# A gated feed-forward layer on one core: a half weight chunk loaded on another DMA queue, and a wide subtraction in three parts

## The chip, the cores and the metric

One core of a Trainium2 chip runs the whole layer in one launch. The metric is the device time of one execution in microseconds. Five engines work side by side, each through its own list of instructions in order: TensorE (PE, matmuls; its weight loads are shown as PEld), VectorE (DVE), ScalarE (ACT), GpSimd (POOL) and SyncE (SP). SyncE and ScalarE also issue the DMA transfers, each on its own queue; an instruction of a list that waits holds up those behind it.

## The reference

x is 2048 x 1024, w_gate and w_up are 1024 x 3584, w_down is 3584 x 1024, all bfloat16:

```
def reference(x, w_gate, w_up, w_down):
    return (gelu(x @ w_gate) * (x @ w_up)) @ w_down      # gelu in its tanh form
```

## The kernel before

The tokens are taken in two halves of 1024 (`for h in range(NH)`, line 972 on), each as two blocks of 512. For a half, the first products give hT, the gelu of the gate times the up product, with the 3584 hidden features on the partitions in 28 tiles of 128; the down products then turn hT into output.

**Products by sums.** The products are not made plainly but in a scheme of seven partial products (Winograd's form of Strassen's), which needs sums and differences of blocks of both factors. A "pair" joins two tiles of 128 features; with the two halves of the contraction and the two blocks of tokens that is a 2 x 2 product of blocks. Its seven products are called m1 to m7. The sums of the weights (s1 to s4, and a22, a plain copy) are made by `s_sum`, on GpSimd for most, on ScalarE for a22, on VectorE for s3 (`s3_both`); the sums of the tokens (t1 to t4, b22) once for a half. In the down products the same is done with hT (`s_down`) and w_down (`t_down`).

**Order of a half.** `quads` (line 498) takes a list of pairs. Per pair PE runs m6, m5, m7, m3, m4 for gate and up, 40 matmuls of 128 x 128 by 128 x 512; while it does so, the sums of the next pair are made (`prep`). m1 and m2 of a pair, plain bfloat16 matmuls of the weight blocks themselves, run ahead of that. The dictionaries `thens` hang further work behind a product of a pair: `thens[7]["m5"]` is done once the code of m5 of the eighth pair has been written, `"start"` before the pair's first product. Each engine's instructions run in the order in which they are written (`on`), so a place in `thens` is a place in each engine's list.

In the first half the order is: `first_units`, a couple of two pairs (MID), the eight LEADS pairs (their m1 and m2 were made in `first_units`), and then the couples from `begin` = 10 on: pairs 10 and 11, then 12 and 13. A couple starts with m1 of both pairs, for each gate then up, so 4 x 4 bfloat16 matmuls, and m2 of both in the same way. "The couple" below is pairs 10 and 11. The second half has seven couples.

**Weight chunks.** `load_w` (line 198) loads columns of w_gate (j = 0) or w_up (j = 1) for a chunk of 512 features, four tiles or two pairs. Chunks lie in two places in turn of `w_mem`, or in still unused parts of hT. Chunk 5 belongs to the couple of pairs 10 and 11: its first half (256 columns) to pair 10, its second to pair 11. It takes the memory of chunk 1, whose second half is read last by the sums of the eighth LEADS pair, which are made during the seventh. Chunk 6 belongs to pairs 12 and 13 and takes the memory of chunk 3. `load_half` (line 1016) loads half a chunk in two transfers, gate then up, 512 KB each; `load_chunk` (line 980) loads a whole one in two of 1024 KB. Both are issued on ScalarE's queue in this stretch.

**What else is on SyncE's queue there.** Two things. (a) The second half's first token block is transposed by DMA into hT, 128 x 512 at a time (`stage_x`, line 736, called through `run_x`, two at a time; six of the eight follow each other in the eighth pair), and stored to DRAM (`store_x`, line 742). (b) The sums t2 and t4 of w_down are made once and kept in DRAM: `stage_load` (line 702) loads two rows' blocks of w_down, `stage_step` (line 719) subtracts on VectorE into one of two buffers in `o_mem`, and line 722 stores the buffer to `t_dram`. A step that writes a buffer waits until the store that reads it has landed.

**A transfer's semaphore.** Each transfer takes the next of eight semaphores in turn, over both queues, and is not issued before the transfer that last used it has landed.

**The down products.** `down_group` starts with m1, 28 bfloat16 matmuls, and then m5, 28 matmuls whose right sides are the 14 blocks of t1, in order, two matmuls a block. For the first group of a half the t1 blocks are made in the last pair's `thens` (lines 1097 to 1121) by `t_down` on VectorE, whose last argument says how many blocks one instruction does: two by default, and six (128 x 3072 elements) for blocks 8 to 13 in the last call (line 1120). The six-block instruction (line 691) is the last of t1; behind it stand the seven in-place subtractions of s2 (line 765).

Of the kernel before, what the change touches and what calls it, by code (L numbers as in the profile page):

```python
# [34 lines left out]
def kernel(  # L35
# [14 lines left out]
    KD = D // P  # L50
# [18 lines left out]
    NS = KF // 2  # L69
# [60 lines left out]
    def sp(inst):  # L130
        return on("sp", inst)

    def act(inst):
        return on("act", inst)

    def dve(inst):
        return on("dve", inst)
# [60 lines left out]
    def load_w(key, j, k0, k1, queue=sp, f0=0, f1=FG):  # L198

        c0 = key[1] * FG  # L200
        eng = nc.scalar if queue is act else nc.sync
        src = (wgv, wuv)[j][:, k0:k1, c0 + f0 : c0 + f1]
        queue(eng.dma_start(out=chunks[key][j][:, k0:k1, f0:f1], in_=src))  # L203
# [24 lines left out]
    FA = 2 * P  # L228
# [391 lines left out]
    def wd_rows(i0, i1):  # L620

        assert i1 <= 8 or i0 >= 8
        e0 = 2 * CH + i0 * D if i1 <= 8 else (i0 - 8) * D
        return w_mem[:, e0 : e0 + (i1 - i0) * D].rearrange("p (a b) -> p a b", b=D)

    def b22_blocks(i0, i1):

        assert i1 <= 4 or i0 >= 4
        e0 = (NS - 8) * D + i0 * DN if i1 <= 4 else 4 * CH + (i0 - 4) * DN
        return w_mem[:, e0 : e0 + (i1 - i0) * DN].rearrange("p (a b) -> p a b", b=DN)  # L630
# [24 lines left out]
    def right(grp, name, i0, i1):  # L655

        r0 = ((grp * len(SEQ) + SEQ.index(name)) * NS + i0) % NR
        assert r0 + i1 - i0 <= NR
        t = t_mem[:, r0 * DN : (r0 + i1 - i0) * DN]
        return t.rearrange("p (a b) -> p a b", b=DN)  # L660
# [16 lines left out]
    def t_down(grp, name, i0, i1, step=2):  # L677

        for i in range(i0, i1, step):
            t = right(grp, name, i, i + step)  # L680
            rows = wd_rows(i, i + step)
            b11, b12 = rows[:, :, 0:DN], rows[:, :, DN:D]
            if name in ("t2", "t4"):
                src = t_dram[:, i : i + step, 0 if name == "t2" else 1, :]
                sp(nc.sync.dma_start(out=t.bitcast(F32), in_=src))
            elif name == "b22":
                act(nc.scalar.copy(out=t, in_=b22_blocks(i, i + step)))
            else:
                b22 = b22_blocks(i, i + step) if name == "t3" else None
                in0, in1 = (b12, b11) if name == "t1" else (b22, b12)  # L690
                dve(nc.vector.tensor_tensor(out=t, in0=in0, in1=in1, op=ALU.subtract))  # L691
# [280 lines left out]
    for h in range(NH):  # L972
        hT = hT0 if h == 0 else hT_pool.tile([P, KF, SH], BF16, name="hT")
        begin = 0
        if h == 0:
# [4 lines left out]
            def load_chunk(key):  # L980
                if key[1] * PPG < NPAIR and key not in chunks:
                    new_chunk(key)
                    for j in range(2):
                        load_w(key, j, 0, KD, act)
# [19 lines left out]
        def run_loads():  # L1004
            while loads and first_step(loads[0]) <= nstep - len(steps):
                stage_load(loads.pop(0))
# [6 lines left out]
        if h == 0:  # L1013
            run_loads()

            def load_half(c, f0):
                if f0 == 0:
                    new_chunk((0, c))
                for j in range(2):
                    load_w((0, c), j, 0, KD, act, f0, f0 + FA)  # L1020

            thens = [
                {
                    "start": [
                        lambda: s_sum(0, MID[0], 0, "a22"),
                        lambda: s_sum(0, MID[0], 1, "a22"),
                        lambda: run_steps(1),
                    ],
                    "m5": [lambda: load_half(3, 0)],
                    "m3": [lambda: run_steps(1)],  # L1030
                    "m4": [lambda: new_x(1), lambda: run_steps(1), run_loads],
                },
                {
                    "m5": [lambda: load_half(3, FA)],
                    "m7": [lambda: fetch_to(QB, 0)],
                    "m3": [lambda: run_steps(1), run_loads],
                },
            ]
            quads(hT, h, MID, (h, LEADS[0]), thens, False, True, True)
            thens = [{} for _ in LEADS]  # L1040
            for n in range(NL):
                thens[n]["start"] = []
                thens[n]["m3"] = [lambda: run_steps(1), run_loads]
            for n in range(NL // 2):
                thens[2 + n]["start"].append(run_x)
            thens[1]["m5"] = [lambda: load_half(4, 0)]
            thens[3]["m5"] = [lambda: load_half(4, FA)]
            thens[5]["m5"] = [lambda: load_half(5, 0)]
            thens[7]["m5"] = [lambda: load_half(5, FA)]
            thens[5]["m7"] = [lambda: load_chunk((0, 6))]  # L1050
            thens[7]["start"].append(run_x)
            thens[7]["m4"] = thens[7]["m3"] + [run_x]
            thens[7]["m7"], thens[7]["m3"] = [run_x], [run_x]
            quads(hT, h, LEADS, (h, begin), thens, True, False, True)
            s_late.append(
                shared_pool.tile([P, NL // 2 * TB], F32R, name="s_late")
            )
            run_late()

        for lead in range(begin, NPAIR, PPG):  # L1060
            members = range(lead, lead + PPG)
            thens = [{} for _ in members]

            def add(n, name, *fs):
                thens[n].setdefault(name, []).extend(fs)

            add(1, "m3", lambda key=(h, lead // PPG + 2): load_chunk(key))
            if h == 0:
                add(0, "m1", lambda: run_steps(2 if lead == begin else 1), run_loads)
                add(0, "start", lambda: run_steps(1), run_loads)  # L1070
                for n in range(PPG):
                    add(n, "m3", lambda: run_steps(1), run_loads)
                    add(n, "m4", run_late)
                if lead == begin:
                    add(0, "m5", lambda: store_x(hT0, 0, KH))
                    add(0, "m3", lambda: store_x(hT0, KH, KD))
                    add(0, "m4", run_late)
            for n, pair in enumerate(members):
                if pair == NPAIR - 2 - (h == 0):
                    add(  # L1080
                        n,
                        "start" if h else "m7",
                        lambda: load_wd_rows(0, 4),
                        lambda: load_wd_rows(4, 8),
                    )
                if h > 0 and 6 < pair < 11:
                    i = s3_late[pair - 7]
                    at = "start" if n == 0 else "m3"
                    add(n, at, lambda i=i: s_down(hT, 0, "s3", i, i + 2))
                if pair < NPAIR - 1:  # L1090
                    continue
                add(
                    0,
                    "m1",
                    lambda: early.append(wd_pool.tile([P, WDT, D], BF16, name="wd_sb")),
                    lambda: s_down(hT, 0, "s3", 0, 4, 4),
                )
                if h == 0:
                    add(0, "m1", lambda: run_steps(1), run_loads)
                add(  # L1100
                    n,
                    "start",
                    lambda: load_b22(4, NS),
                    lambda: load_wd_rows(8, 10),
                    lambda: load_wd_rows(10, 12),
                    lambda: load_wd_rows(12, NS),
                    lambda: load_b22(0, 4),
                )
                add(n, "m6", lambda: t_down(0, "t1", 4, 6))
                add(n, "m7", lambda: s_down(hT, 0, "s1", 4, 8, 4))  # L1110
                add(n, "m7", lambda: s_down(hT, 0, "s1", 0, 4, 4))
                add(n, "m3", lambda: t_down(0, "t1", 0, 2))
                add(
                    n,
                    "m4",
                    lambda: t_down(0, "t2", 0, NT2),
                    lambda: t_down(0, "t1", 2, 4),
                    lambda: t_down(0, "t1", 6, 8),
                    lambda: s_down(hT, 0, "s1", 8, NS, 6),
                    lambda: t_down(0, "t1", 8, NS, 6),  # L1120
                )
            nxt = (h, lead + PPG) if lead + PPG < NPAIR else None
            quads(hT, h, members, nxt, thens, lead == 0)
# [78 lines left out]
```

## Time and profile before

| | us |
|---|---|
| median of 3 runs | 540.74 |
| lowest, highest | 540.11, 541.68 |
| the profiled execution | 542.03 |
| its span, first to last instruction | 540.3 |
| PE busy in it | 532.3 |

The granted clock of TensorE is 1.000 over the span. Moments are given in microseconds from the span's start. In the views, L511 is the line of the pairs' matmuls, L793 that of the down products' matmuls; "w_mem<-in_w_up_dram" reads: written is w_mem, read is w_up. A row of the timeline gives start, duration, engine, line, operation, tiles, shapes, the count of instructions merged into it, and in brackets the idle time before and what ended it. A row of the waits gives the total in us, the number of waits and the longest.

### The profile page before, as it was taken

To read this page: it belongs to the slowest core of one execution; us is meant where nothing else is said; L and a number is where in the kernel's file an instruction comes from. 1 tells how busy PE (TensorE), PEld (TensorE's weight loads), DVE (VectorE), ACT (ScalarE), POOL (GpSimd) and SP (SyncE) were. 2 spreads that over 40 slices of the span, in tenths; PEclk is the share of its full clock that TensorE was granted. 3 is DMA by queue.
4 is the path that set the end of the run, shared out by engine and by line. 5 is a ranking of instruction groups with operands and counts; after the bars stand their busy time and mean duration, and the time that the engine had idled before them with its cause. 6 is when DMAs were issued, how large, how long until landed. Compare 5 with 4: busy or idle time off the path is not lost.

```text
span 540.3 us, 6965 instructions
## 1 busy us (share of the span) xinstructions
PE 532.3 (99%) x2360; PEld 382.1 (71%) x2380; DVE 374.8 (69%) x453; ACT 273.8 (51%) x471; POOL 256.7 (48%) x202
## 2 busy tenths in 40 slices
PE   9999999999899999999999999999999999999997
PEld 4448888876577676767768676776768686866866
DVE  0399988989599998889565253434444569969951
ACT  4466666656454319216465555556555551452270
POOL 0079999997399300000045494948677670000000
PEclk9999999999999999999999999999999999999999
DMA  8974747399982896789950413314050329677845
GB/s 221 249 269 118 234 153 183 90 296 195 288 287 106 293 341 226 252 267 307 324 189 4 153 51 107 103 54 150 7 156 13 143 86 339 217 246 241 292 143 209
DMA packets 97747, 102.69 MB, mean 190 GB/s; under 512 B 18224, under 2 KB 72624, under 8 KB 97712
## 3 DMA queue, kind: packets, MB, share of 16 engines
q1 hardware_dynamic: 71248, 82.52, 48.2%
q10 hardware_dynamic: 26464, 19.73, 12.9%
q8 instruction: 19, 0.31, 0.2%
q14 instruction: 16, 0.13, 0.1%
HBM read 85.98 MB, written 12.58 MB: 182 GB/s over the span
## 4 chain that ended last, share of the span: by engine, by line
PE 95%; DMA 4%; issue 1%; DVE 0%; ACT 0%; DVEq 0%; ACTq 0%
PE bank L511 57%; PE bank L793 33%; PE bank L355 5%; DMA w_mem<-in_w_up_dram 2%; DMA hT<-in_w_gate_dram 1%; DMA t_dram<-o_sb 1%; DMA w_mem<-in_x_dram 1%; DVE o_sb L719 0%; DVE hT L318 0%; ACT o_sb L849 0%; DVEq L318 0%; ACTq L203 0%
## 5 line engine op out<-in xcount | busy, mean ns | idle before, releaser
L511 PE MATMUL bank<-t_mem,s_mem 128*128 128x512 f32 x1096 | 252.5, 391 | 0.0
L511 PEld LDWEIGHTS bank<-t_mem,s_mem 128*128 128x128 f32 x1096 | 205.6, 188 | 44.2 <-ACT bank L572 0.9
L462 POOL TENSOR_TENSOR s_mem<-w_mem 128x512 fp32r<-128x512 bf16 x80 | 100.4, 1274 | 180.6 <-DVE t_mem L300 95.5
L318 DVE TENSOR_TENSOR hT<-w_mem,bank 128x512 bf16<-128x512 f32 x106 | 71.2, 683 | 73.2 <-PE bank L511 43.5
L527 DVE TENSOR_TENSOR bank<-bank,m 128x512 f32<-128x512 f32 x112 | 72.4, 693 | 45.2 <-ACT m L567 42.7
L793 PE MATMUL bank<-t_mem,s_mem 128*128 128x512 f32 x416 | 98.8, 394 | 0.1
L313 ACT ACTIVATE w_mem<-bank 128x512 f32<-128x512 f32 x106 | 62.8, 596 | 59.1 <-DVE bank L527 35.7
L793 PEld LDWEIGHTS bank<-t_mem,s_mem 128*128 128x128 f32 x416 | 78.0, 188 | 18.0 <-DVE t_mem L691 0.9
L511 PE MATMUL bank<-xT,w_mem 128*128 128x512 bf16 x311 | 70.5, 379 | 3.0 <-DMA w_mem<-in_w_up_dram 2.5
L462 POOL TENSOR_TENSOR s_mem<-w_mem,s_mem 128x512 fp32r<-128x512 bf16 x46 | 65.6, 1448 | 3.4 <-PE bank L511 3.4
L691 DVE TENSOR_TENSOR t_mem<-w_mem 128x1024 fp32r<-128x1024 bf16 (+1 forms) x52 | 65.7, 1307 | 0.4 <-PE bank L511 0.4
L511 PEld LDWEIGHTS <-w_mem 128*128 128x128 bf16 x320 | 30.5, 98 | 40.8 <-DMA w_mem<-in_w_up_dram 3.0
L462 POOL TENSOR_TENSOR s_mem<-s_mem,w_mem 128x512 fp32r<-128x512 f32 x46 | 55.7, 1231 | 0.2
L572 ACT COPY bank<-bank 128x512 f32<-128x512 f32 x56 | 32.0, 571 | 25.8 <-PE bank L511 21.5
L475 ACT CAST s_mem<-w_mem 128x512 fp32r<-128x512 bf16 x48 | 29.5, 616 | 24.8 <-PE bank L511 23.5
L567 ACT COPY m<-bank 128x512 f32<-128x512 f32 x56 | 32.9, 588 | 16.1 <-PE bank L511 16.0
L793 PEld LDWEIGHTS <-hT 128*128 128x128 bf16 x224 | 21.3, 98 | 26.6 <-issue 2.1
L858 ACT CAST o_sb<-bank 128x512 bf16<-128x512 f32 x27 | 14.8, 585 | 33.8 <-PE bank L793 33.8
L793 PE MATMUL bank<-t_mem,s_late 128*128 128x512 f32 (+1 forms) x132 | 30.3, 382 | 0.0
L537 ACT COPY bank<-bank 128x512 f32<-128x512 f32 x40 | 22.8, 570 | 14.7 <-PE bank L511 14.7
L765 DVE TENSOR_TENSOR s_mem<-hT 128x512 fp32r<-128x512 bf16 (+2 forms) x28 | 23.0, 838 | 8.6 <-PE bank L793 8.6
L793 PEld LDWEIGHTS bank<-t_mem,s_late 128*128 128x128 f32 x132 | 24.4, 188 | 4.9
(61 smaller groups left out, 397.3 us busy)
## 6 DMA issues: line engine op xcount, KB each, us to landing
t_mem<-t_dram SPq DMA_DIRECT2D x56, 512.0 KB, 5.5
wd_sb<-in_w_down_dram SPq DMA_DIRECT2D x26, 512.0 KB, 7.3
t_dram<-o_sb SPq DMA_DIRECT2D x14, 512.0 KB, 3.2
w_mem<-in_w_gate_dram ACTq DMA_DIRECT2D x6, 1024.0 KB, 5.4
w_mem<-in_w_up_dram ACTq DMA_DIRECT2D x6, 1024.0 KB, 7.9
w_mem<-in_w_gate_dram SPq DMA_DIRECT2D x8, 512.0 KB, 6.0
w_mem<-in_w_up_dram SPq DMA_DIRECT2D x8, 512.0 KB, 7.3
w_mem<-in_w_down_dram SPq DMA_DIRECT2D x4, 1024.0 KB, 6.7
```

The source lines that it names most:

```text
L313: act(nc.scalar.activation(out=g_sb, in_=ps[:], func=ACT.Gelu_apprx_tanh))
L318: nc.vector.tensor_tensor(out=hT[:, fc, tb * TB : (tb + 1) * TB], in0=g_sb, in1=ps[:], op=ALU.mult,)
L355: nc.tensor.matmul(banks[held[u][j]][:], lhsT=w_sb[:, kd, f0 : f0 + P], rhs=xT[0][:, kd, :], start=kd == 0, stop=kd in (KH - 1, KD - 1), s ...
L462: pool(nc.gpsimd.tensor_tensor(out=t, in0=in0, in1=in1, op=op))
L475: act(nc.scalar.copy(out=t, in_=a(1, 1)))
L511: nc.tensor.matmul(banks[bank][:], lhsT=lhs[:, c, :], rhs=rhs[:, c, :], start=start and c == 0, stop=c == KH - 1, skip_group_check=True,)
L527: nc.vector.tensor_tensor(out=banks[dst][:], in0=banks[src][:], in1=m5[:], op=ALU.add)
L567: act(nc.scalar.copy(out=m5[j][:], in_=banks[V_[j]][:]))
L572: act(nc.scalar.copy(out=banks[R_[j]][:], in_=banks[Q_[j]][:]))
L691: dve(nc.vector.tensor_tensor(out=t, in0=in0, in1=in1, op=ALU.subtract))
L765: dve(nc.vector.tensor_tensor(out=t, in0=in0, in1=in1, op=op))
L793: nc.tensor.matmul(banks[bank][:, c0:c1], lhsT=lhs(i, u), rhs=rhs(i)[:, c0:c1], start=start and i == 0, stop=stop and i == NS - 1, skip_gr ...
```

## The change

`load_half` gets the queue as an argument. The second half of chunk 5 is issued on SyncE's queue at the start of the eighth LEADS pair, ahead of that pair's first transposes, and no longer on ScalarE's after that pair's m5. Chunk 6 is issued on ScalarE's queue after m5 of the seventh pair, no longer after m7 of the sixth. And the last `t_down` call of t1 does two blocks an instruction, three instructions in place of one, in both halves of the tokens. The order of all other instructions on PE, DVE, ACT and POOL stays.

```diff
-            def load_half(c, f0):
+            def load_half(c, f0, queue=act):
                 if f0 == 0:
                     new_chunk((0, c))
                 for j in range(2):
-                    load_w((0, c), j, 0, KD, act, f0, f0 + FA)
+                    load_w((0, c), j, 0, KD, queue, f0, f0 + FA)
...
             thens[5]["m5"] = [lambda: load_half(5, 0)]
-            thens[7]["m5"] = [lambda: load_half(5, FA)]
-            thens[5]["m7"] = [lambda: load_chunk((0, 6))]
+            thens[7]["start"].append(lambda: load_half(5, FA, sp))
+            thens[6]["m5"] = [lambda: load_chunk((0, 6))]
             thens[7]["start"].append(run_x)
...
                     lambda: s_down(hT, 0, "s1", 8, NS, 6),
-                    lambda: t_down(0, "t1", 8, NS, 6),
+                    lambda: t_down(0, "t1", 8, NS),
```

## The prediction

> **What bounds the kernel now.** I read the page's first rows, then the chain of work that ended last, then the waits by engine, then the timelines around the places these point at.
>
> ```profile
> span 540.3 us, 6965 instructions
> PE 532.3 (99%) x2360; PEld 382.1 (71%) x2380; DVE 374.8 (69%) x453; ACT 273.8 (51%) x471; POOL 256.7 (48%) x202
> ```
>
> The span is TensorE's: 532.3 of 540.3 us. Only the 8.0 us in which PE has nothing to multiply can be won, and the edit removes no matmul. Which of these 8 us does it touch? The waits name two candidates.
>
> ```profile
> PE bank L511 <- DMA w_mem<-in_w_up_dram: 2.5, 1, 2.5
> PEld bank L793 <- DVE t_mem L691: 0.9, 2, 0.5
> ```
>
> The first is one wait of 2.5 us for a load of w_up, the second two waits of the weight load for the helper whose call is split, one in each half of the tokens. The chain shows where the first comes from (start, duration, what):
>
> ```profile
> 124.95 3.17 DMA t_dram<-o_sb
> ...
> 128.14 0.02 ACTq L203
> ...
> 128.20 8.86 DMA w_mem<-in_w_up_dram
> ...
> 137.10 22.89 PE bank L511 x101
> ```
>
> The up half of the couple's second half chunk is issued at 128.20, only after a store on SyncE's queue has landed (124.95 to 128.12), takes 8.86 us, and PE starts as it lands. The PE timeline gives the hole's size:
>
> ```profile
> 99.73 32.25 PE L511 MATMUL bank<-t_mem,s_mem 128*128 128x512 f32 x139
> 131.82 2.76 PE L511 MATMUL bank<-xT,w_mem 128*128 128x512 bf16 x11
> 137.10 4.49 PE L511 MATMUL bank<-xT,w_mem 128*128 128x512 bf16 x20 [2.52 <-DMA w_mem<-in_w_up_dram]
> 141.25 18.52 PE L511 MATMUL bank<-t_mem,s_mem 128*128 128x512 f32 x80
> ```
>
> The third row's 20 matmuls at 0.38 us each overlap: (4.49 - 0.38) / 19 = 0.216 us from start to start. The last matmul before the hole ends at 131.82 + 2.76 = 134.58, so starts at 134.20, and the next was due at 134.42. It starts at 137.10: the stall costs **2.68 us**. By the same pace the gate half, which feeds the four matmuls just before, is needed at 134.42 - 4 x 0.216 = 133.56.
>
> **The change part by part.** What issues when, on ScalarE's queue (first six rows) and on SyncE's (the rest):
>
> ```profile
> 107.94 0.37 ACTq L203 DMA_DIRECT2D w_mem<-in_w_gate_dram  x1
> 108.41 0.77 ACTq L203 DMA_DIRECT2D w_mem<-in_w_up_dram  x1
> 109.82 1.58 ACTq L203 DMA_DIRECT2D w_mem<-in_w_gate_dram  x1
> 111.44 2.22 ACTq L203 DMA_DIRECT2D w_mem<-in_w_up_dram  x1
> 126.63 0.37 ACTq L203 DMA_DIRECT2D w_mem<-in_w_gate_dram  x1
> 128.20 0.39 ACTq L203 DMA_DIRECT2D w_mem<-in_w_up_dram  x1
> ...
> 116.81 0.38 SPq L702 DMA_DIRECT2D wd_sb<-in_w_down_dram  x1
> 124.95 0.37 SPq L722 DMA_DIRECT2D t_dram<-o_sb  x1
> 125.42 10.03 SPq L736 DMA_TRANSPOSE hT<-in_x_dram  x6
> 135.54 0.53 SPq L722 DMA_DIRECT2D t_dram<-o_sb  x1
> ...
> 137.33 2.54 SPq L736 DMA_TRANSPOSE hT<-in_x_dram  x2
> ```
>
> *The half chunk moves to SyncE's queue.* Its two issues (the fifth and sixth row) now stand between the store at 124.95 and the six transposes. They read and write the same memory, so they wait for the same last GpSimd subtraction, which already let the queue go on here (the transposes start at 125.42 with no gap after the store). The gate half is then issued at 125.42 and the up half near 125.8, 1.2 and 2.4 us earlier, and ahead of the transposes, where until now the up half was issued beside the third of them. In the built program the up half no longer waits for the store's landing but for a transfer issued near 108, long over.
>
> When does it land? The rates of two-microsecond stretches (last two columns: share of the DMA engines, GB/s):
>
> ```profile
> 121.00:123.00 2.00, 2.00 (x11) 1.65 (x10) 2.00 (x2) 2.00 (x5) 2.00 (x2) 1.00 1.07 369
> 131.00:133.00 2.00, 1.95 (x10) 1.07 (x10) 2.00 (x5) 1.73 (x4) 2.00 (x2) 1.00 1.39 276
> 133.00:135.00 2.00, 1.58 (x8) 0.50 (x6) 2.00 (x3) 1.36 (x3) 0.28 (x1) 1.00 1.55 67
> ```
>
> Undisturbed loads move at some 350 GB/s (the first row, taken 5% lower). The whole chunk comes one pair later, near 118, so from there to the end of the half chunk lie one w_down load (0.52 MB), the whole chunk (2.10), the store (0.52) and the half chunk (1.05): 4.19 MB, 12.0 us at 350 GB/s. The way there and back adds some 1.6, what the smallest store takes in all:
>
> ```profile
> out_dram<-o_sb SPq DMA_DIRECT2D x1, 64.0 KB, 1.6
> ```
>
> That is **131.6**. The other bound comes from the nearest like transfers, the half chunks (512 KB) and the whole chunk (1024 KB) of this stretch, median us from issue to landing:
>
> ```profile
> w_mem<-in_w_gate_dram ACTq DMA_DIRECT2D x2, 512.0 KB, 5.6
> w_mem<-in_w_up_dram ACTq DMA_DIRECT2D x2, 512.0 KB, 8.7
> w_mem<-in_w_gate_dram ACTq DMA_DIRECT2D x1, 1024.0 KB, 10.1
> w_mem<-in_w_up_dram ACTq DMA_DIRECT2D x1, 1024.0 KB, 13.0
> ```
>
> Up half 125.8 + 8.7 = 134.5, gate half 125.4 + 5.6 = 131.0: against 134.42 and 133.56, so even that leaves 0.1 us. I take 131.6, nearer to what the order in the queue gives; the stall goes whole: **-2.68 us** (bounds -2.6 and -2.68 by these rows, 0 and a loss by the rivals).
>
> A page speaks against this. The Trainium skill, DMA: Bandwidth & Descriptors, section "Issuing engines are not separate DMA queues", says that DMAs of either engine run on the same 16 DMA engines and interleave, whoever started them, so that another issuing engine saves little but sequencer time. By it the change of queue as such would bring nothing, only the earlier issue and the place ahead of the transposes; the third rival gives its time.
>
> *The whole chunk, one pair later.* Its two issues took 1.58 and 2.22 us (third and fourth row) behind the unfinished half chunk of 107.94, and held ScalarE's queue up to 113.66. One pair later nothing is ahead of them, and 0.4 us each is likely. ScalarE gains up to 3 us there, PE nothing: the 139 matmuls from 99.73 run without an idle entry at (32.25 - 0.39) / 138 = 0.231 us, against (18.52 - 0.39) / 79 = 0.230 in the stretch from 141.25. The bound is 138 x 0.001 = 0.2 us; I take 0. The chunk is first read, by the preparation of the pair after next, in the couple's second pair, half way through the 80 matmuls from 141.25, near 150.5; issued at 118 and at the 13.0 us of its row it lands by 132. That is cover enough.
>
> *What is queued behind on SyncE.* Two issues of 0.4 us push the six transposes, the store and the load behind them by 0.8 us. Who waits for these? VectorE, in its subtraction of the staged w_down, which writes a buffer that the store of 135.54 reads:
>
> ```profile
> 142.31 1.22 DVE L719 TENSOR_TENSOR o_sb<-wd_sb,o_sb 128x1024 fp32r<-128x1024 bf16 x1
> 145.00 0.70 DVE L527 TENSOR_TENSOR bank<-bank,m 128x512 f32<-128x512 f32 x1 [1.48 <-ACT m L567]
> ```
>
> ```profile
> t_dram<-o_sb SPq DMA_DIRECT2D x1, 512.0 KB, 4.2
> ```
>
> The last row is that store: 135.54 + 4.2 = 139.8. PE needs the sum of 145.00 at its 25th matmul after 141.25, near 146.9; in the changed kernel, 2.68 earlier, 144.2. So the sum must start by 143.5, the subtraction by 142.3, and the store must have landed then: 2.5 us later than now, against 0.8 of issue. Cost 0; the first rival prices what lies beyond.
>
> *One subtraction split in three* (both halves of the tokens, from line 1120). First its duration and that of the narrow form, then the first place where PE waits for it:
>
> ```profile
> L691 DVE TENSOR_TENSOR t_mem<-w_mem 128x1024 fp32r<-128x1024 bf16 x50 | 59.0, 1225 | 0.4 <-PE bank L511 0.4
> ```
>
> ```profile
> 191.19 3.35 DVE L691 TENSOR_TENSOR t_mem<-w_mem 128x3072 fp32r<-128x3072 bf16 x1
> 462.50 3.48 DVE L691 TENSOR_TENSOR t_mem<-w_mem 128x1024 fp32r<-128x1024 bf16 x3
> ...
> 190.55 4.03 PE L793 MATMUL bank<-t_mem,s_mem 128*128 128x512 f32 x16
> 194.59 5.58 PEld L793 LDWEIGHTS bank<-t_mem,s_mem 128*128 128x128 f32 x25 [0.44 <-DVE t_mem L691]
> ```
>
> The wide one ends at 194.54, and the 17th weight load starts at 194.59: rows 8 to 13 of t1 were all one wait. Three narrow ones in a row take 3.48 us, as at 462.50: the first is done at 191.19 + 1.22 = 192.4, the second at 193.6, the third at 194.7. PE wants the 17th matmul at 190.55 + 16 x 0.230 = 194.2, the 21st at 195.2, the 25th at 196.1: none waits. The matmul was due at 194.2 and could start at 194.6, and a weight load that stands idle 0.44 us leaves the next one uncovered too; I take **0.3 us** for each place, between 0 and 0.45. VectorE works 0.13 us longer; its next subtractions, seven in 4.3 us, stay ahead of a PE that uses a pair in 0.9. Two places: **-0.6 us**.
>
> **Sum:** 2.68 + 0.6 = 3.3 us. The profiled execution took 542.03 us (span 540.3 and 1.7 around it), so the changed one would take 538.7. The median of the three runs is 540.74, 1.29 lower. If profiling adds these 1.29 to any run, the median goes to 537.4. But the last rate row shows 67 GB/s against 276 just before: the landing at 137.06 includes a pause of about (276 - 67) x 2 / 276 = 1.5 us, which other runs need not have; then their stall is nearer 1.2 to 1.4, the gain 1.8 to 2.0, and the median 538.7 to 538.9. The three runs' spread, 540.11 to 541.68, is as wide as such a pause. I stand between, at the side of the pause: **538.4 us**, own range 537.3 to 539.2.
>
> **The rivals.**
> 1. *SyncE's queue becomes late.* If the transposes can't be issued until the half chunk has drained (131.6), six at 1.3 us end at 139.4 (the last row of SyncE's queue: two took 2.54; the six here took 10.03, their end in the pause), the store lands at 143.6 and the subtraction misses its 142.3 by 1.3 us. For it: an issue behind queued work did stretch (2.22 us at 111.44). Against it: these transposes were issued beside the half chunk too. Price 1.3, net -2.0: 538.7 to 540.0.
> 2. *The stall is small in ordinary runs* (the edit does what it says, where little is to be had). With the pause and the slow stretch after it gone, the up half lands at 135 and the stall is 0.6; with the split's 0.6 the gain is 1.2: 539.5. For it the 67 GB/s row; against it the range of three runs.
> 3. *The half chunk shares the engines as before.* From the gate's issue to the up half's landing it took 137.06 - 126.63 = 10.43 us; from 125.42 that is 135.85, and 1.43 us of stall stay. Net -1.25 - 0.6: 540.2 in the profiled run's terms, 538.9 to 540.2. By the Trainium skill (DMA: Bandwidth & Descriptors, "Issuing engines are not separate DMA queues") this is the case. The trace, with an up half issued beside the third transpose, can't tell.
> 4. *Slower: the whole chunk gets in front.* It is now issued at 118, not 110, so the half chunk may find 2.1 MB ahead of it. The up half at the 13.0 us that the whole chunk's up part took behind other loads lands at 125.8 + 13.0 = 138.8: a stall of 4.4 for 2.68, less 0.6, is +1.1: 541.8. It decides from a landing at 137.7 on; at over 0.3% only from 139.3 on. Against it: by the volumes above the whole chunk is through at 127.
>
> **How the numbers follow.** Forecast 0.62, rival 1 0.08, rival 2 0.14, rival 3 0.08, rival 4 0.08. A measurement of this kernel can tell about 0.3%, 1.6 us, from no change: the bounds are 539.1 and 542.4. Nearly all of the forecast, with half of rival 1, is faster: 0.64. Rivals 2 and 3, the rest of rival 1 and part of 4: same, 0.30. Slower 0.06. The range goes from 537.2 to 540.3: it leaves out rival 4 and the edges.
>
> **What would show it.** Right: no PE wait for w_up left near 134; the up half's landing before 134.4; no weight load waiting for L691; three L691 rows of 1.2 us in place of one of 3.35; PE idle time down from 8.0 to about 5 us. Wrong: a wait of PE or the weight load at 134 to 148 for w_gate, w_up or for VectorE behind a store; a landing after 134.4; the m5 of the down stage waiting for a later subtraction.

## The result and the profile after

The changed kernel takes 537.68 us (median of 6 runs, 537.35 to 539.00), the kernel before beside it 541.49 (6 runs, 540.11 to 543.21): a ratio of 0.9935, 95% interval 0.9914 to 0.9955. The profiled execution took 538.38 us for 542.03.

The first rows of the page after, then PE's waits:

```profile
span 536.6 us, 6968 instructions
...
PE 531.6 (99%) x2360; PEld 382.4 (71%) x2380; DVE 375.8 (70%) x457; ACT 274.2 (51%) x471; POOL 257.9 (48%) x202
```

```profile
PE bank L245 <- PEq L1186: 0.8, 1, 0.8
PE bank L793 <- DMA t_mem<-t_dram: 0.2, 1, 0.2
```

PE runs the same 2360 matmuls; 5.0 us are idle in place of 8.0, and w_up is no longer among its waits. The timeline of PE (start, duration, count) shows where the hole was:

```profile
99.77 31.89 PE L511 MATMUL bank<-t_mem,s_mem 128*128 128x512 f32 x140
131.51 7.08 PE L511 MATMUL bank<-xT,w_mem 128*128 128x512 bf16 x31
138.24 18.51 PE L511 MATMUL bank<-t_mem,s_mem 128*128 128x512 f32 x80
```

m1 and m2 of the couple are one row now. From the first of these matmuls to the first of m6 it is 138.24 - 131.51 = 6.73 us, against 141.25 - 131.82 = 9.43 before. SyncE's queue, and the landing of the two halves after their issue:

```profile
125.03 0.37 SPq L722 DMA_DIRECT2D t_dram<-o_sb  x1
125.48 0.42 SPq L203 DMA_DIRECT2D w_mem<-in_w_gate_dram  x1
126.00 1.02 SPq L203 DMA_DIRECT2D w_mem<-in_w_up_dram  x1
127.07 10.23 SPq L736 DMA_TRANSPOSE hT<-in_x_dram  x6
137.40 0.53 SPq L722 DMA_DIRECT2D t_dram<-o_sb  x1
```

```profile
w_mem<-in_w_gate_dram SPq DMA_DIRECT2D x1, 512.0 KB, 5.8
w_mem<-in_w_up_dram SPq DMA_DIRECT2D x1, 512.0 KB, 7.3
```

The up half lands at 126.00 + 7.3 = 133.3, 0.8 us before PE (131.51 + 12 x 0.216 = 134.1) wants it. VectorE does meet the queue's delay, without harm:

```profile
140.92 1.23 DVE L719 TENSOR_TENSOR o_sb<-wd_sb,o_sb 128x1024 fp32r<-128x1024 bf16 x1 [1.54 <-DMA t_dram<-o_sb]
142.06 1.53 DVE L527 TENSOR_TENSOR bank<-bank,m 128x512 f32<-128x512 f32 x2
```

And the split: three narrow subtractions, and 55 weight loads beside them without an idle entry:

```profile
188.18 3.49 DVE L691 TENSOR_TENSOR t_mem<-w_mem 128x1024 fp32r<-128x1024 bf16 x3
```

```profile
187.51 12.47 PEld L793 LDWEIGHTS bank<-t_mem,s_mem 128*128 128x128 f32 x55
```

The spans differ by 3.66 us. Taking the starts of PE's instructions in each trace (first matmul of line 511, first of the couple's m1, first of its m6, first of each down stage, first of the second half's pairs) and the end of its last one cuts every execution into the same stages, and this table carries most of what follows (us):

| run | start | to the couple | m1, m2 | to down | down 1 | second half's pairs | down 2 | tail |
|---|---|---|---|---|---|---|---|---|
| before | 33.65 | 98.17 | 9.43 | 43.44 | 88.25 | 175.56 | 88.42 | 3.34 |
| changed | 33.89 | 97.62 | 6.73 | 43.43 | 87.89 | 175.56 | 88.55 | 2.91 |
| e1, split only | 33.40 | 98.22 | 10.81 | 43.45 | 87.98 | 175.58 | 88.15 | 3.34 |
| e2, half only | 33.63 | 98.23 | 6.73 | 43.43 | 88.26 | 175.56 | 88.45 | 2.93 |
| e3, chunk only | 33.59 | 97.61 | 9.97 | 43.45 | 88.25 | 175.56 | 88.45 | 3.34 |
| e4, half on ScalarE's queue | 34.01 | 97.62 | 6.73 | 43.43 | 87.89 | 175.56 | 88.10 | 3.34 |
| e5, transposes later | 33.74 | 98.21 | 6.73 | 46.04 | 88.25 | 175.56 | 88.57 | 3.34 |
| e6, whole chunk in front | 33.81 | 97.62 | 12.75 | 43.45 | 87.89 | 175.56 | 88.09 | 3.36 |
| e7, plain copies | 33.56 | 98.27 | 8.20 | 43.42 | 88.21 | 175.56 | 88.60 | 3.33 |
| e9, behind two transposes | 33.75 | 97.59 | 7.49 | 43.43 | 88.20 | 175.56 | 88.10 | 2.92 |

The start (32.9 to 34.1 over all runs) and the tail (2.9 or 3.3) vary whatever the kernel. What "m1, m2" has above 6.73 is a stall on weights and, in e1 and e6, a lower clock after it.

"To the couple" is 0.55 us shorter in the changed kernel, where the prediction took nothing. This row of the waits before, which stands next to the one for L691 and has the same total, is gone from the changed kernel's waits:

```profile
PEld bank L511 <- ACT bank L572: 0.9, 2, 0.5
```

The two are weight loads that waited for a copy of ScalarE, at 116.85 and 118.09 in the kernel before. They are gone in every kernel below that moves the whole chunk, and one or two such waits stand there in every kernel that doesn't.

### The profile page after: what moved, and what is told of

It is laid out like the page before. It is cut to its first block, busy times and chain, and to the rows that moved or that the text cites. A ratio compares the mean times of both kernels' runs of the same rounds, so it can differ in the third digit from the quotient of the medians.

```text
span 536.6 us, 6968 instructions
## 1 busy us (share of the span) xinstructions
PE 531.6 (99%) x2360; PEld 382.4 (71%) x2380; DVE 375.8 (70%) x457; ACT 274.2 (51%) x471; POOL 257.9 (48%) x202
## 4 chain that ended last, share of the span: by engine, by line
PE 98%; DMA 1%; issue 0%; ACT 0%
PE bank L511 60%; PE bank L793 31%; PE bank L355 5%; DMA t_mem<-t_dram 1%; PE bank L245 1%; PE bank L337 0%; ACT o_sb L849 0%
## 5 line engine op out<-in xcount | busy, mean ns | idle before, releaser
L691 DVE TENSOR_TENSOR t_mem<-w_mem 128x1024 fp32r<-128x1024 bf16 x56 | 66.6, 1236 | 0.9 <-PE bank L511 0.9
L572 ACT COPY bank<-bank 128x512 f32<-128x512 f32 x56 | 32.0, 571 | 26.5 <-PE bank L511 21.2
```

The lines of the kernel that those rows point to most:

```text
L572: act(nc.scalar.copy(out=banks[R_[j]][:], in_=banks[Q_[j]][:]))
```

## The experiments

Each kernel is timed beside the kernel before on the same chip.

**The three parts one by one.** e2 moves the half chunk alone (`load_half` has the queue as an argument here too):

```diff
-            thens[7]["m5"] = [lambda: load_half(5, FA)]
+            thens[7]["start"].append(lambda: load_half(5, FA, sp))
```

> The kernel before with the second half of chunk 5 alone moved to SyncE's queue ahead of the transposes; the whole chunk and the wide subtraction as before. Theory A: both halves land near 131 to 133, the stall is gone, -2.7 us: about 538.8; steps of PE above 0.3 us near 117 to 118 stay, since ScalarE is still held up by the whole chunk's issue. Rival C (it is the whole chunk's move that frees the half): the up half lands after 134.4 and over 1 us of stall stays, 540 or more.

Measured: 538.45 us for 541.33, ratio 0.9940 (0.9919 to 0.9961). The up half's landing in e2, and PE:

```profile
w_mem<-in_w_up_dram SPq DMA_DIRECT2D x1, 512.0 KB, 5.9
```

```profile
131.86 7.08 PE L511 MATMUL bank<-xT,w_mem 128*128 128x512 bf16 x31
```

No stall: the move of the half chunk alone takes it away, as theory A had it; rival C falls. "To the couple" stays at 98.23, and so do the two waits of the weight load for L572.

e1 splits the subtraction alone (the last diff line of the change).

> The kernel before with the subtraction of t1 alone split in three. Theory A (the forecast's: the stall on the up half belongs to the half chunk's loads, the split is worth what the two weight-load waits show): the two waits of the weight load for L691 go, PE gains 0.33 to 0.36 us at each of the two places, 0.7 together, and the stall of about 2.7 us near 134 stays; median about 540.8 for 541.5 before. Rival B (the longer VectorE chain costs what the earlier start gives, since seven subtractions stand behind it): within 0.2 us of before, with a new wait of PE for L765 in m6 of the down stage.

Measured: 540.57 for 541.33, ratio 0.9985 (0.9971 to 1.0000). The difference of the medians is 0.76 where 0.7 was expected, at the edge of what the runs resolve. The trace has 87.98 and 88.15 for the down stages, 0.27 each below the kernel before, and no weight load waits for L691. But its m1 and m2 took longer than in the kernel before: PE, and its granted clock (next to last column) in two-microsecond stretches:

```profile
131.62 2.76 PE L511 MATMUL bank<-xT,w_mem 128*128 128x512 bf16 x11
136.60 6.18 PE L511 MATMUL bank<-xT,w_mem 128*128 128x512 bf16 x20 [2.22 <-DMA w_mem<-in_w_up_dram]
```

```profile
135.00:137.00 2.00, 0.40 (x2) 0.96 1.05 132
137.00:139.00 2.00, 2.00 (x7) 0.50 1.11 378
139.00:141.00 2.00, 2.00 (x8) 0.68 1.17 347
```

The stall is 2.4 us here, but the 20 matmuls after it take 6.18 us where the kernel before needed 4.49: the clock fell to 0.50 after the stall, which cost another 1.7 us.

e3 moves the whole chunk alone:

```diff
-            thens[5]["m7"] = [lambda: load_chunk((0, 6))]
+            thens[6]["m5"] = [lambda: load_chunk((0, 6))]
```

> The kernel before with the whole chunk alone moved one pair later; the half chunk stays on ScalarE's queue behind m5 of the eighth pair. In the built order the up half then waits for the whole chunk's gate load instead of SyncE's store. Theory A: the up half is issued near 127.1 instead of 128.2 and still shares the DMA engines with the transposes, lands near 135.5 to 136.5, 1 to 2 us of stall stay; with the 0.5 us that ScalarE's delay cost PE near 117, -1.2 to -2.2: 539.3 to 540.3. Rival C: stall gone, 538.3.

Measured: 540.55 for 541.33, ratio 0.9988 (0.9970 to 1.0006), so no gain that the runs resolve, where 1.2 to 2.2 us were expected. In e3 the up half was issued at 126.48, 1.7 us earlier than in the kernel before, and landed no earlier, 10.5 us after:

```profile
w_mem<-in_w_up_dram ACTq DMA_DIRECT2D x1, 512.0 KB, 10.5
```

```profile
137.03 3.19 PE L511 MATMUL bank<-xT,w_mem 128*128 128x512 bf16 x14 [3.07 <-DMA w_mem<-in_w_up_dram]
```

The stall is longer than the expected 1 to 2 us. So an earlier issue alone, beside the second transpose, gains nothing. What e3 gains ahead of the couple, 98.17 to 97.61, it loses in the couple, 9.43 to 9.97: PE arrives earlier for a load that lands at the same time.

**Queue or moment.** e4 issues the half at the changed kernel's place, on the other queue:

```diff
-            thens[7]["start"].append(lambda: load_half(5, FA, sp))
+            thens[7]["start"].append(lambda: load_half(5, FA, act))
```

> The changed kernel with the half chunk issued at the same place of the program but on ScalarE's queue, so at 123.7 to 125.4 and on another queue than the transposes. Rival D (the queue does not matter, only the time of issue; the transfers interleave anyway): the up half takes 7 to 7.5 us from its issue as in the changed kernel, no stall, 537.7. Theory A (the place ahead of the transposes in one queue matters): the half shares the engines with the transposes and takes 8.7 to 10.4 us, landing at 132.5 to 135, stall 0 to 0.6: 537.7 to 538.3, and the transposes land earlier than in the changed kernel.

Measured: 537.64, ratio 0.9928 (0.9908 to 0.9947), the changed kernel's time. In e4 the loads go out 2 us earlier, since ScalarE's queue doesn't wait for the store, and the up half lands at 132.3:

```profile
122.94 0.37 ACTq L203 DMA_DIRECT2D w_mem<-in_w_gate_dram  x1
124.07 0.44 ACTq L203 DMA_DIRECT2D w_mem<-in_w_up_dram  x1
```

```profile
w_mem<-in_w_up_dram ACTq DMA_DIRECT2D x1, 512.0 KB, 8.2
```

The time fits both, the 8.2 us of transfer lie between them. SyncE's queue as such isn't needed: issued ahead of the transposes, and here about 2 us earlier as well, the half is in time on ScalarE's queue too.

e9 puts the half behind the first two transposes on SyncE's queue, so as late as in the kernel before:

```diff
-            thens[7]["start"].append(lambda: load_half(5, FA, sp))
             thens[6]["m5"] = [lambda: load_chunk((0, 6))]
             thens[7]["start"].append(run_x)
+            thens[7]["start"].append(lambda: load_half(5, FA, sp))
```

> The changed kernel with the half chunk on SyncE's queue behind the first two of the six transposes, so issued near 128.1 and 128.6, as late as in the kernel before (126.6 and 128.2), but still ahead of the other four in the same queue. Theory G (what made the up half late is the transposes that shared the engines with it, and a place ahead of most of them cures it whatever the moment of issue): the up half lands 5 to 6 us after its issue, at 133.6 to 134.8, stall 0 to 0.4: 537.7 to 538.2. Rival H (the 2.4 us of earlier issue are what counts): it takes 7.3 us as in the changed kernel, lands near 136, a stall of 1.5 stays: 539.2 or more.

Measured: 538.63 for 541.22, ratio 0.9941 (0.9922 to 0.9960). The up half was issued at 128.73, half a microsecond later than before, and took 5.9 us:

```profile
w_mem<-in_w_up_dram SPq DMA_DIRECT2D x1, 512.0 KB, 5.9
```

```profile
134.69 4.49 PE L511 MATMUL bank<-xT,w_mem 128*128 128x512 bf16 x20 [0.54 <-DMA w_mem<-in_w_up_dram]
```

The stage is 7.49, a stall of 0.76 where the kernel before had 2.70, though PE gets there 0.5 us earlier than before. e3, with the whole chunk at the same place and the half beside the transposes on the other queue, issued the up half 2.25 us earlier and stalled 3.2 us. So about 2 us of the stall were the transposes that shared the way, and the 0.7 that stay are put down to the moment of issue by difference: nearer to G than to H, though beyond G's 0.4.

**The transposes.** e5 is the kernel before again: it leaves the half chunk alone and issues all eight transposes behind m4:

```diff
-            thens[7]["start"].append(run_x)
-            thens[7]["m4"] = thens[7]["m3"] + [run_x]
-            thens[7]["m7"], thens[7]["m3"] = [run_x], [run_x]
+            thens[7]["m4"] = thens[7]["m3"] + [run_x] * 4
+            thens[7]["m3"] = []
```

> The kernel before with all eight transposes of the second half's x tokens moved behind m4 of the eighth pair, so behind the half chunk's loads; half chunk, whole chunk and subtraction as before. Theory A (the transposes in flight beside the half chunk, and the pauses of all 16 DMA engines that come while they drain, make the up half late, not its issue as such): issued near 127.1 it lands at 132 to 133.5, no stall, median near 538.6 as with the half chunk moved, and a spread of about 1 us in place of 3.5. Rival E (the half is issued too late at that place whatever lies beside it): it lands after 134.4 and 1 us or more of stall stays, 539.7 or more.

Measured: 542.58 for 541.20, ratio 1.0023 (1.0009 to 1.0036): slower. The first half of the expectation holds: with nothing beside it the up half took 5.1 us, landed at 132.3, and m1 and m2 took 6.73. The other half fails. SyncE, VectorE and PE in e5:

```profile
135.50 10.69 SPq L736 DMA_TRANSPOSE hT<-in_x_dram  x8
146.71 0.38 SPq L722 DMA_DIRECT2D t_dram<-o_sb  x1
```

```profile
149.97 2.03 DVE L719 TENSOR_TENSOR o_sb<-wd_sb 128x1024 fp32r<-128x1024 bf16 x1 [2.87 <-DMA t_dram<-o_sb]
```

```profile
153.41 1.17 PE L511 MATMUL bank<-t_mem,s_mem 128*128 128x512 f32 x4 [0.76 <-ACT bank L572]
155.91 3.89 PE L511 MATMUL bank<-t_mem,s_mem 128*128 128x512 f32 x16 [1.33 <-DVE bank L527]
```

Eight transposes in a row hold SyncE's queue for 10.7 us; the store behind them lands late, VectorE's subtraction waits 2.87 us for it, its sums come late, and PE waits: "to down" grows from 43.44 to 46.04, by 2.6, what the stall had cost. One loss takes the place of the other, which would leave the time as it was; but the median is another 1.4 us worse. Part of this goes with the clock: four of the eleven runs had a granted clock of 0.996 or 0.997 over the span, and they are the four longest (543.25 to 544.56). The other seven, with a median of 542.23, are still 1.0 us above the kernel before, and the one trace doesn't say why.

e7 puts plain copies of the same bytes in the transposes' places (`dma_start` for `dma_start_transpose` in line 736, from rows of 1 KB). It leaves out the transposition, so only its time means anything.

> The kernel before with the eight transposes of the second half's first x block replaced by plain copies of the same bytes at the same places (128 rows of 1 KB each, so the second half's products of that block are of other numbers; time alone is read). Theory A: without transposes no pause of 1 us or more falls between 125 and 138, the up half lands 6 to 7 us after its issue at 128.2, so at 134.2 to 135.2, stall 0 to 0.8: median 538.5 to 539.5, with a narrow spread. Rival F (the pauses belong to the traffic or to the memory, not to the transposes): pauses and a stall of 1 to 3 us stay, 540 to 541.5.

Measured: 541.15 for 541.20, ratio 0.9997 (0.9989 to 1.0006), spread 540.39 to 541.57. PE, and two stretches of DMA (share of the engines, GB/s), in e7:

```profile
135.89 1.47 PE L511 MATMUL bank<-xT,w_mem 128*128 128x512 bf16 x6 [1.30 <-DMA w_mem<-in_w_up_dram]
```

```profile
131.00:133.00 2.00, 1.95 (x10) 1.07 (x10) 2.00 (x5) 1.72 (x4) 2.00 (x2) 1.00 1.09 337
133.00:135.00 2.00, 1.59 (x8) 0.50 (x6) 2.00 (x3) 1.36 (x3) 0.29 (x1) 1.00 0.60 170
```

The pause is gone: no stretch here has engines busy with little moved, as the kernel before had at 133 (a share of 1.55 at 67 GB/s). The up half still took 7.8 us after 128.06, and 1.47 us of stall stay. So theory A is half right: without transposes the pauses are gone and the spread is narrower (1.2 us, against 2.9 for the kernel before beside it); but plain traffic beside the half (six copies of 128 KB) makes it late too, and the median does not move. The time and the stall are those of rival F, without its reason. The copies also go out faster than the transposes, all six within 3.3 us in place of 10.0, so e7 changes more than the pauses. Its trace has the stage 1.23 us shorter than the kernel before's; why the median shows nothing of this, one trace doesn't say.

**The rival that was to be slower.** e6 issues the whole chunk on SyncE's queue just ahead of the half:

```diff
-            def load_chunk(key):
+            def load_chunk(key, queue=act):
...
-                        load_w(key, j, 0, KD, act)
+                        load_w(key, j, 0, KD, queue)
...
+            thens[7]["start"].append(lambda: load_chunk((0, 6), sp))
             thens[7]["start"].append(lambda: load_half(5, FA, sp))
-            thens[6]["m5"] = [lambda: load_chunk((0, 6))]
```

> The changed kernel with the whole chunk issued on SyncE's queue just ahead of the half chunk, at the start of the eighth pair: 2.1 MB more in front of the half, the fourth rival of the prediction made real. By the volumes: 2.1 MB at 350 GB/s is 6 us, the up half lands at 133.3 + 6 = 139, a stall of about 4.8 us, and the transposes and the store behind come 3 to 6 us later, so VectorE's subtraction may add up to 1.5: median 542 to 544. If the half instead passes or shares with the whole chunk: landing before 136, 538 to 539.5.

Measured: 544.90 for 541.20, ratio 1.0066 (1.0050 to 1.0082), above the 542 to 544 expected. PE in e6 waits for the gate half, issued at 127.03 and landed at 137.7, and the clock falls again:

```profile
137.72 2.74 PE L511 MATMUL bank<-xT,w_mem 128*128 128x512 bf16 x6 [4.38 <-DMA w_mem<-in_w_gate_dram]
```

```profile
137.00:139.00 2.00, 1.28 (x4) 0.57 1.47 102
139.00:141.00 2.00, 2.00 (x7) 0.57 0.75 160
```

The stall is near what the volumes gave, about 4.5 us; the stage is 6.0 us longer than the changed kernel's, so 1.5 are the clock's, which the expectation had not. VectorE's delay adds nothing ("to down" stays at 43.45).

**What the two small parts are worth.** e8 is the changed kernel with the whole chunk back at its old place; in a last round e10 (the wide subtraction back), e11 (the changed kernel) and e12 (as e8) ran side by side, all three without a stall in m1.

> The changed kernel with the whole chunk back at its old place: half chunk on SyncE's queue and the split alone. Theory A with the correction that ScalarE, held up by the whole chunk's issue behind the unfinished half chunk, cost PE 0.5 us near 117: the steps of PE above 0.3 us near 117 to 118 come back and the median is 538.1 to 538.3, 0.4 to 0.6 above the changed kernel. Rival (that hold-up is covered, as the prediction had it): 537.7, as the changed kernel.

> The changed kernel with the subtraction of t1 wide again: half chunk and whole chunk moved, no split. It is timed beside the changed kernel and the one without the whole chunk's move, where no stall on the up half blurs the comparison. Theory A: the two weight-load waits for L691 are back, 0.35 us each, so 0.7 us above the changed kernel of the same job, about 538.4 for 537.7. Rival B (the split gives back what it gains): within 0.2 us of the changed kernel.

> The changed kernel itself, as the base for the other two of this job: 537.4 to 538.0, no stall at the couple's m1, granted clock 1.00 throughout.

> The changed kernel with the whole chunk at its old place once more, now beside the changed kernel on one chip. Theory A with the correction: 0.55 to 0.6 us above the changed kernel, all of it before the couple's m1. Rival: the 0.9 us between the medians of the two earlier jobs, of which the trace would show only 0.6.

| run | median us | ratio to before | to the couple | down 1 | down 2 |
|---|---|---|---|---|---|
| e8 | 538.59 | 0.9948 (0.9936 to 0.9960) | 98.22 | 87.89 | 88.09 |
| e10 | 538.20 | 0.9947 (0.9933 to 0.9962) | 97.59 | 88.25 | 88.42 |
| e11 | 537.73 | 0.9938 (0.9924 to 0.9951) | 97.81 | 88.68 | 88.09 |
| e12 | 537.85 | 0.9944 (0.9929 to 0.9958) | 98.19 | 87.92 | 88.09 |

e10 is 0.47 above e11: in the direction of theory A, less than its 0.7. The traces give the split 0.36 + 0.33 (88.25 to 87.89, 88.42 to 88.09). The whole chunk's move is 0.9 us between e8 and the changed kernel of the first round, but 0.12 between e12 and e11, so neither median is where it was expected; the traces have 0.4 to 0.6. e11's profiled run lost 0.8 in down 1 to a late load of t2, as the changed kernel's first lost 0.45 in down 2: losses of that size come and go, and the medians of five or six runs don't resolve these two parts. They rest on the traces. The mechanism of the second shows in the traces, in e12 for one:

```profile
109.23 1.51 ACTq L203 DMA_DIRECT2D w_mem<-in_w_gate_dram  x1
110.78 1.98 ACTq L203 DMA_DIRECT2D w_mem<-in_w_up_dram  x1
```

```profile
117.51 13.90 PE L511 MATMUL bank<-t_mem,s_mem 128*128 128x512 f32 x60 [0.29 <-ACT bank L572]
```

ScalarE's gelu stands behind the issue that ends at 112.76, its later copies slip, and PE waits for one of them (the changed kernel's row from 99.77 has no such wait).

## Why the prediction was right, point by point

- **The stall goes whole: right.** Forecast 2.68 us, measured 9.43 - 6.73 = 2.70, and e2 shows that the half chunk's move alone does it. The forecast landing of 131.6 was 1.7 us early: a pause (112 GB/s at a share of 1.56 in 131 to 133) fell into it, and 0.8 us of slack remained. The whole chunk's move works against the half: the chunk was still in flight when the half was issued at 125.5, and the up half took 7.3 us; in e2, with the chunk at its old place, it took 5.9.
- **Why it goes: partly right.** The text laid it to an earlier issue and a place ahead of the transposes. e9 and e3 divide it: the place about 2 us, the moment by difference 0.7, and none of it where the earlier issue still runs beside transposes. In e5, with nothing beside it, the up half took 5.1 us; from the old moment, 128.20, that would be 133.3 by this estimate, in time for 134.42. That the up half waited for the store's landing was true and hardly mattered (e3 does without it and gains nothing).
- **The split: right.** Forecast 0.3 a place, measured 0.36 and 0.33 between e10 and the traces of the other kernels with the split that lost nothing to a late load, 0.27 at each place in e1.
- **The whole chunk's move at nothing: wrong.** Forecast 0 with a bound of 0.2, from a pace averaged over 138 matmuls; measured 98.17 - 97.62 = 0.55. The cover taken for granted, that PE doesn't feel ScalarE's delay, wasn't whole. The text read PE's matmul row alone, which has no idle entry, and named two candidates among the waits; the third, the weight load's 0.9 us for L572, was there to be read in the same way as the 0.9 us for L691. The pace didn't show it because the comparison stretch starts slowly itself (its first step takes 0.42 us where the others take 0.23).
- **The behaviour on SyncE's queue: right in its cost of nothing, too small in the delay.** Two issues of 0.4 us were to push the rest by 0.8; they took 0.42 and 1.02, the transposes began 1.65 us later than before, the store 1.9 later. It landed at 140.8, VectorE waited 1.54 us, and its subtraction started at 140.92 against the limit of 142.3. e5 shows the mechanism of rival 1 real beyond it.
- **The sum:** 2.70 + 0.55 + 0.36, less 0.24 at the start and 0.13 in down 2 (0.33 gained, 0.45 lost to a late load), and 0.43 in the tail, make the 3.66 of the spans to 0.01. Start, tail and the late load are not the edit's doing; its parts come to 2.70 + 0.55 + 0.36 + 0.33 = 3.9. The prediction's 3.3 lacked the 0.55.
- **From the profiled run to the median: wrong side, and the nearness is part luck.** The working's own choice was between 537.4 and 538.9 and leaned to a stall of 1.2 to 1.4 us in ordinary runs, which "need not have" the pause. e7 has about that stall without the pause (1.47). But the pause is no accident of one run: each of the traces of e1, e2, e3, e8, e9 and the changed kernel, with transposes draining beside the half, has such a stretch too (a share of 1.55 to 1.91 at 85 to 185 GB/s). And e2, which takes away this stall alone, gained 541.33 - 538.45 = 2.88. So the forecast gain of 540.74 - 538.4 = 2.3 is too small against the measured 3.8. The forecast time is off by only 0.7 because it started from a median of three runs that lay 0.75 below that of six (541.49), an error the other way. The direction is clear: the upper bound of the ratio, 0.9955, lies beyond the 0.3% that the text took to be resolvable.
- **What the text had not: the clock.** e1 shows that a stall of this length can also drop the clock. In the kernel before's own trace it did not. Of the 66 runs of the kernel before that were timed beside the experiments, seven had a granted clock of 0.996 or 0.997 over the span, and took 542.6 to 543.5 us; the others had 0.999 or 1.000, with a longest of 543.14. Half the clock for 3.4 us is 0.003 of the span, and 1.7 us, so these seven fit e1, though only e1 and e6 were traced in this condition. None of the 59 runs of the changed kernel, e2, e4 and e7 to e12 had it. Over the 66 runs it is worth some 0.2 us in the mean.
- **Rival 2** falls with e2's 2.88. **Rival 3** is refuted: from the gate's issue to the up half's landing it took 133.3 - 125.5 = 7.8 us, not 10.4. The rule it leant on stands, though. The Trainium skill, DMA: Bandwidth & Descriptors, "Issuing engines are not separate DMA queues", has transfers of either queue interleave on the same engines; e4, at the changed kernel's time from the other queue, agrees with it. What I had drawn from it, that the half would be as slow, left out that the transposes came later. **Rival 4** has its mechanism in e6, and the length of its stall (4.4 forecast, about 4.5 measured), but not its price: e6 is 3.7 us slower than the kernel before, not 1.1. Its condition did not occur: by 127.0 the whole chunk had landed.

## What to carry to other kernels

When a load is late, look at what is issued just ahead of it and beside it on all queues before moving it earlier: here the place ahead of most of a run of transposes was worth about 2 us, the earlier moment 0.7. Then follow the queue that takes it in, instruction by instruction, to the engine that waits behind: 1.6 us of delay on the queue here, harmless, and ten in e5, which gave back all that was won. When you ask what PE waits for, read the rows of its weight loads (PEld) beside those of its matmuls: the 0.55 us that the prediction missed stood only there. And a gap of 2 to 3 us on PE can cost more than its length, when the clock drops after it, as in some of the runs here.

## What the runs showed of the hardware that was not expected

- **The clock after a stall.** After a stall of 2.4 us the granted clock was 0.50 for some 3.4 us (e1: its three rows lack 0.04, 0.50 and 0.32 of 2 us each), after 4.5 us for about as long (e6); after 2.7 (before) and 3.2 us (e3) it stayed at 1.00. The Trainium skill, TensorE: Matmul & The Clock Gate, "Part 1: The HAM clock gate", says that the clock falls to half after at least one idle window of about 3.4 us, and that the window runs freely. That it depends on the moment agrees with these four; that it needs 3.4 us of idleness does not agree with e1, where it fell after 2.4, and there the measurement decides.
- **Pauses of the DMA engines while transposes drain beside loads**: a share of 1.55 at 67 GB/s in the kernel before, 1.56 at 112 in the changed one (the share adds up the packets' times, so it can pass 1). There is none with plain copies, and none in e5, where the eight transposes drain with little beside them (a share of at most 1.04 from 135 to 149). What holds the packets up, no run here shows.
- **Issues behind unfinished transfers can take longer**: the whole chunk's two issues took 1.51 and 1.98 us behind an unfinished half chunk (e12). How much must lie ahead, no run here shows: in e4 the half's issues took 0.37 and 0.44 us while the whole chunk, landed at 127.4, was unfinished on the same queue. In the changed kernel, with nothing ahead, the whole chunk's took:

```profile
117.20 0.37 ACTq L203 DMA_DIRECT2D w_mem<-in_w_gate_dram  x1
117.62 0.60 ACTq L203 DMA_DIRECT2D w_mem<-in_w_up_dram  x1
```
